# A cached-attention and gated-FFN decode step: kept V tiles, matmuls on constants, and a new last stage

## The chip, the core and the metric

The kernel runs on one core of a Trainium2 chip. The core has five engines that run side by side: PE (TensorE, matrix products), DVE (VectorE, elementwise work and small transposes), ACT (ScalarE, exp and tanh), POOL (GpSimd) and SP (SyncE, which issues the DMAs). The metric is device time in microseconds (us). The time before is 311.15 us, the median of 13 runs (308.57 to 312.18).

## The reference

Four sequences of one token each go twice through the same attention layer and the same feed-forward layer, with the same weights and the same key and value caches.

```python
# B=4 sequences, D=512; 32 query heads, 8 K/V heads, cache length 4096, head size 128; F=1792
def A(x, k_cache, v_cache, wq, wo):
    q = (x @ wq) as [B, 32, 1, 128]
    p = softmax(q @ k^T * 128**-0.5)          # each K/V head serves 4 query heads
    return (p @ v) as [B, 1, 4096] @ wo
def B(x, w_gate, w_up, w_down):
    return (gelu(x @ w_gate) * (x @ w_up)) @ w_down
x = x + A(layernorm(x)); x = x + B(layernorm(x))
x = x + A(layernorm(x)); x = x + B(layernorm(x))
```

Everything is bf16 in memory. One K or V cache is 4 x 8 x 4096 x 128 numbers, 33.6 MB; the weights are 13.9 MB.

## The kernel before

The program is ordered by hand: each engine runs its instructions in the order in which the code names them, and SP issues all DMAs from one queue (`dq`), where an issue that waits for a buffer holds up all later ones.

*Tiles.* The cache of one element (sequence) and one K/V head is cut into two tiles of 128 x 16 x 128, 512 KB each; so K and V have 16 tiles each per element. `KT` has 16 buffers, one for each K tile of an element. V rotates through seven buffers (`KV_BUFS`, `free`), and `held` says which tile lies where.

*Passes.* Each element needs two attention passes, with a feed-forward stage (`dense`) after each. Element b's K tiles are loaded once: they are turned by DVE (L375, `turn`), used for the scores of the first pass, and stay until the scores of the second pass have read them (`scores`, L386). Only then are the buffers loaded with the K tiles of element b+1 (`keys.load`, L368). V is read twice, once in each pass. V tiles are used in the order `order`: all 16 of the first pass of element 0; then for each b the first four of b's second pass, the 16 of the first pass of b+1 and the other twelve of b's second pass; at the end the second pass of element 3. `Values.step` uses one V tile: 16 matmuls of 128 x 32 (L485); then it frees the buffer and calls `load_v` (L464), which asks for the next tiles in that order as long as a buffer is free. `keep` names V tiles that are not freed after the first pass and not loaded again: `KEEP` = 2 tiles, of element 0 only (L450). The first two tiles of a second pass are the last two of the first pass of the same element.

*Stages.* `attend(None, 0)` is the first pass of element 0; all weights are loaded behind its V tiles (`load_rest`: wo in four pieces, wg, wu, and wd in three pieces of 7, 4 and 3 of its 14 columns of blocks). The loop over b then runs `dense(b, 1, ...)`, the feed-forward stage of one element, builds the queries of its second pass, and calls `attend(b, b+1)`: the scores of b's second pass, the loads of K of b+1, and the first pass of b+1. In the dense stages of elements 1 to 3, `fill` steps through the twelve V tiles of the second pass of the element before, between the pieces of the dense stage; in that of element 0 it does nothing. `attend_last` is the second pass of element 3; eight of its V tiles go into K buffers that are free by then. The second feed-forward layer runs once, for all four elements, as `dense(0, B, ...)`, and after it the result is cast, transposed by four matmuls into PSUM (L715), copied (L717) and written out (L718).

*Inside a dense stage:* the end of the output projection (L287), the residual (L294 or L298), the layer norm's sums through one matmul with a constant matrix (L170, L177: the statistics matmul), the reciprocal root by ten small DVE instructions (`ln_rstd`, L186 to L201), the gate and up products (L315 for one element, L308 for four), gelu (L325 to L332, tanh on ACT at L331), `gate_up` (L338, L341), and the down projection (L349, 56 matmuls).

`ROWS` are two PSUM banks for products that come out as rows; `new_scores(0)` and `new_scores(1)` are the two banks of scores.

Of the kernel before, what the change touches and what calls it, by code (L numbers as in the profile page):

```python
# [15 lines left out]
P = 128  # L16
# [3 lines left out]
QD = 4  # L20
# [10 lines left out]
def kernel(  # L31
# [58 lines left out]
    wd_sb = wts.tile([P, KF, D], BF16, name="wd_sb")  # L90
    KT = [[wts.tile([P, CH, Dh], BF16, name=f"kt{i}_{t}") for t in range(NT)] for i in range(Hkv)]
    wq_dram = A_wq.rearrange("(k p) n -> p k n", p=P)
# [6 lines left out]
    q1_bf = state.tile([P, NG, NK, B], BF16, name="q1_bf")  # L99
    xn_bf = state.tile([P, KD, B], BF16, name="xn_bf")  # L100
    qb = state.tile([P, W + NK * 2 * W], BF16, name="qb")

# [12 lines left out]
    def groups(b):  # L115
        return [b % NG, (b + 1) % NG]

    def cache_tile(cache, b, kvh, t):
        return cache[b, kvh].rearrange("(p c) d -> p c d", p=P)[:, t * CH:(t + 1) * CH]

# [4 lines left out]
    def load_rest():  # L125
        n = Hq // 4
        for i in range(4):
            dq.dma_start(out=wo_sb[:, i * n:(i + 1) * n], in_=wo_dram[:, i * n:(i + 1) * n])  # L128
        dq.dma_start(out=wg_sb[:], in_=B_w_gate.rearrange("(k p) n -> p k n", p=P))  # L129
        dq.dma_start(out=wu_sb[:], in_=B_w_up.rearrange("(k p) n -> p k n", p=P))  # L130
        wd_dram = B_w_down.rearrange("(k p) n -> p k n", p=P)
        cuts = [0, KF // 2, KF - 3, KF]
        for lo, hi in zip(cuts, cuts[1:]):
            dq.dma_start(out=wd_sb[:, lo:hi], in_=wd_dram[:, lo:hi])  # L134

    def build_consts():
        nc.vector.memset(mean_f[:], 1.0 / D)
        nc.vector.memset(magic[:], 0x5F3759DF)
        for r in ROWS:
            nc.vector.memset(r[:], 0.0)  # L140
        nc.vector.memset(qb[:], 0.0)
        nc.vector.tensor_reduce(out=amask[:], in_=ident_bf[:].rearrange("p (a i) -> p a i", a=QD),
                                axis=AX.X, op=ALU.max)
        nc.vector.tensor_reduce(out=s32_f[:], in_=ident_bf[:].rearrange("p (a i) -> p i a", a=QD),
                                axis=AX.X, op=ALU.max)
        nc.vector.tensor_copy(out=t32_bf[:],
                              in_=s32_f[:].unsqueeze(1).broadcast_to([P, QD, QS]))
        nc.vector.tensor_reduce(out=hmask[:], in_=s32_f[:].rearrange("p (y h) -> p h y", h=rep),
                                axis=AX.X, op=ALU.max)
        nc.vector.scalar_tensor_tensor(  # L150
            out=dmask[:], in0=amask[:].unsqueeze(2).broadcast_to([P, GH, rep]), scalar=float(D),
            in1=hmask[:].unsqueeze(1).broadcast_to([P, GH, rep]), op0=ALU.mult, op1=ALU.mult)
# [147 lines left out]

    def ffn_in(b0, nb, w_sb, cols):
        bs = slice(b0, b0 + nb)
        rows = new_rows()
        if cols:
            h = rows[:, :KF * nb].rearrange("p (c j) -> p c j", j=nb)
            for c in range(KF):
                for k in range(KD):
                    nc.tensor.matmul(h[:, c], lhsT=w_sb[:, k, c * P:(c + 1) * P],  # L308
                                     rhs=xn_bf[:, k, bs], start=(c == 0 and k == 0),
                                     stop=(k == KD - 1), skip_group_check=True)  # L310
            return h, cols
        for k in range(KD):
            w = w_sb[:, k].rearrange("p (n a i) -> p a n i", a=QD, i=QS)
            for j in range(QD):
                nc.tensor.matmul(rows[j * QS:j * QS + nb, :KF * QS], lhsT=xn_bf[:, k, bs],  # L315
                                 rhs=w[:, j], start=(k == 0), stop=(k == KD - 1))
        return rows, cols

    def ffn_cols(h, nb):
        return h[0] if h[1] else turn_rows(h[0], KF * QS)[:, :, :nb]  # L320

    def gelu(nb, rows, rstd):
        hg = ffn_cols(rows, nb)
        h = small.tile([P, KF, nb], FP32, name="h", tag="h")
        nc.vector.tensor_tensor(out=h[:], in0=hg, in1=spread_rstd(rstd, KF, nb), op=ALU.mult)  # L325
        sq = small.tile([P, KF, nb], FP32, name="sq", tag="sq")
        nc.vector.scalar_tensor_tensor(out=sq[:], in0=h[:], scalar=0.044715, in1=h[:],
                                       op0=ALU.mult, op1=ALU.mult)
        nc.vector.scalar_tensor_tensor(out=sq[:], in0=sq[:], scalar=1.0, in1=h[:],  # L329
                                       op0=ALU.add, op1=ALU.mult)  # L330
        nc.scalar.activation(out=sq[:], in_=sq[:], func=ACT.Tanh, scale=GELU_C)  # L331
        nc.vector.scalar_tensor_tensor(out=h[:], in0=h[:], scalar=0.5,  # L332
                                       in1=spread_rstd(rstd, KF, nb), op0=ALU.mult, op1=ALU.mult)
        return sq, h

    def gate_up(nb, sq, h, rows):
        hu = ffn_cols(rows, nb)
        nc.vector.scalar_tensor_tensor(out=sq[:], in0=sq[:], scalar=1.0, in1=h[:],  # L338
                                       op0=ALU.add, op1=ALU.mult)
        H_bf = small.tile([P, KF, nb], BF16, name="H_bf", tag="H_bf")  # L340
        nc.vector.tensor_tensor(out=H_bf[:], in0=hu, in1=sq[:], op=ALU.mult)  # L341
        return H_bf

    def down(nb, H_bf):
        n = WIDE * rep // nb
        y = ps_sm.tile([P, KD, n, nb], FP32, name="y", tag="sm")
        for c in range(KF):
            for k in range(KD):
                nc.tensor.matmul(y[:, k], lhsT=wd_sb[:, c, k * P:(k + 1) * P],  # L349
# [5 lines left out]
    class Keys:  # L355
# [3 lines left out]
        def tile(self, n):  # L359
            o, u = divmod(n, TG)  # L360
            t, s = divmod(u, GH)
            return groups(self.b)[o] * GH + s, t

        def load(self, count):
            for _ in range(count):
                kvh, t = self.tile(self.nl)
                self.nl += 1
                dq.dma_start(out=KT[kvh][t][:], in_=cache_tile(A_k_cache, self.b, kvh, t))  # L368

# [79 lines left out]
    order += value_order(B - 1, 1)  # L449
    keep = {(0,) + u[2:] for u in value_order(0, 1)[:KEEP]}  # L450
    VB = Hkv * NT
# [5 lines left out]
    def load_v():  # L457
        while free and seen["load"] < seen["upto"]:
# [4 lines left out]
            v = held[b, g, s, t] = free.pop(0)  # L463
            dq.dma_start(out=v[:], in_=cache_tile(A_v_cache, b, g * GH + s, t))  # L464

# [36 lines left out]
    def attend(b2, b1, next_q=None, rest=None):  # L502
# [40 lines left out]
        else:  # L543
            load_wq(0)
            keys.load(TG)
            load_wq(1)
            keys.load(TG)
            load_v()
# [9 lines left out]
            build_q1(0, 0)  # L558
            turn(4)
        sc1 = new_scores(0)  # L560
        scores(sc1, ga, 0)
        turn(4)
        if two:
            vals2.step(max(early[b2] - vals2.n - 1, 0))
        scores(sc1, ga, 1)
        turn()
        p0 = soft(sc1)
# [6 lines left out]
        prob1[ga] = (pe, soft_recip(den))  # L574
        if first:
            q_first(q_rows(0, B, 1), 1, rstd1)
        build_q1(b1, gb)
        turn()
        vals.step(2)
        sc1 = new_scores(0)  # L580
        scores(sc1, gb, 0)
        turn(4)
        vals.step(3)
# [19 lines left out]
        if first:  # L603
# [7 lines left out]
            return (y, OT_bf, heads[3], hp), vals2  # L611
        vals.step(2)
        out_proj(rows, OT_bf, heads[2], hp)
        vals.step()
        out_proj(rows, OT_bf, heads[4], rep, False, True)
        yc = y_rows(rows, 1)
        vals.step()
        y = y_select(yc, 1)
        vals.step()
        return (y, OT_bf, heads[5], rep), vals2  # L620
# [42 lines left out]

    def dense(b0, nb, proj, fill):
        out_proj_end(*proj)
# [5 lines left out]
        fill(1)  # L671
        rg = ffn_in(b0, nb, wg_sb, nb > 1)
        fill(1)
        ru = ffn_in(b0, nb, wu_sb, nb > 1)
        sq, h = gelu(nb, rg, ln_rstd(nb, mv))
        H_bf = gate_up(nb, sq, h, ru)
        fill(2)
        add_y(b0, nb, down(nb, H_bf))

# [3 lines left out]
    for b in range(B):  # L683
        fill = (lambda n: None) if prev is None else prev.step
        dense(b, 1, proj, fill)
        ln_square(b, 1)
# [21 lines left out]

    dense(0, B, proj, lambda n: None)

    xoT = state.tile([P, KD, B], BF16, name="xoT")
    nc.vector.tensor_copy(out=xoT[:], in_=XX[:, 0].rearrange("p b k -> p k b"))
    xo_ps = ps_sm.tile([P, D], BF16, name="xo_ps", tag="sm")
    for k in range(KD):
        nc.tensor.transpose(xo_ps[:B, k * P:(k + 1) * P], xoT[:, k, :], ident_bf[:, :])  # L715
    xo = tmpp.tile([P, D], BF16, name="xo", tag="pp")
    nc.vector.tensor_copy(out=xo[:B, :], in_=xo_ps[:B, :])  # L717
    nc.sync.dma_start(out=out.flatten_outer_dims(), in_=xo[:B, :])  # L718

# [29 lines left out]
```

## Time and profile before

| What | Value |
|---|---|
| median of 13 runs | 311.15 us (308.57 to 312.18) |
| the profiled execution's own time | 311.93 us |
| its span, first to last instruction | 310.2 us |
| mean granted clock of PE | 0.73 of full |
| busy: PE, DVE, ACT | 198.2 us, 170.8 us, 29.1 us |
| DMA | 114.09 MB, mean 368 GB/s |
| issues of K tiles, of V tiles | 64, 118 + 8 of 512 KB |

The profile tells of one execution. A row of the groups gives line, engine, operation, what it writes and reads, how often, busy time, the mean of one in ns, and the engine's idle time ahead of it with what ended it:

```profile
L485 PE MATMUL ot<-pe,v 128*128 128x32 bf16 x1920 | 65.1, 183 | 23.4 <-DMA v<-in_A_v_cache_dram 21.4
L375 DVE STREAM_TRANSPOSE kt<-kt 128x1024 f32<-128x1024 f32 x64 | 75.2, 1217 | 7.1 <-DMA kt<-in_A_k_cache_dram 6.9
...
L386 PE MATMUL sc<-kt,qb 128*32 128x512 bf16 x512 | 55.3, 481 | 17.4 <-DVE kt L375 13.6
```

Busy time says how long an engine had something in work, not how long the program waited for it; PE's matmuls overlap, so the mean of one is longer than the distance from one to the next. The span is told in slices (a digit is a share in tenths), in stretches of time with busy time, granted clock, DMA share and GB/s, and as a chain that is followed back from the last instruction to what released each step.

### The profile page before, as it was taken

To read this page: it belongs to the slowest core of one execution; us is meant where nothing else is said; L and a number is where in the kernel's file an instruction comes from. 1 tells how busy PE (TensorE), PEld (TensorE's weight loads), DVE (VectorE), ACT (ScalarE), POOL (GpSimd) and SP (SyncE) were. 2 spreads that over 40 slices of the span, in tenths; PEclk is the share of its full clock that TensorE was granted. 3 is DMA by queue.
4 is the path that set the end of the run, shared out by engine and by line. 5 is a ranking of instruction groups with operands and counts; after the bars stand their busy time and mean duration, and the time that the engine had idled before them with its cause. 6 is when DMAs were issued, how large, how long until landed. Compare 5 with 4: busy or idle time off the path is not lost.

```text
span 310.2 us, 8714 instructions
## 1 busy us (share of the span) xinstructions
PE 198.2 (64%) x3844; PEld 117.7 (38%) x3844; DVE 170.8 (55%) x481; ACT 29.1 (9%) x70; POOL 0.7 (0%) x6
## 2 busy tenths in 40 slices
PE   1360475343577458788864469799553776997975
PEld 0110244211323125556431346465311454645654
DVE  5585751014247987455588934455598642555143
ACT  0003001000002020300100112000102040003000
POOL 0000000000000000000000000000000000000000
PEclk9999997555558958859955585579755795679685
DMA  7999999999949999999999999999999999999910
GB/s 247 398 412 394 404 411 406 357 367 398 378 165 341 397 413 407 409 405 408 407 408 408 409 407 393 384 389 388 356 413 409 411 408 405 380 362 371 411 76 3
DMA packets 35526, 114.09 MB, mean 368 GB/s; under 512 B 3224, under 2 KB 9120, under 8 KB 35488
## 3 DMA queue, kind: packets, MB, share of 16 engines
q1 hardware_dynamic: 35488, 113.53, 95.0%
q8 instruction: 30, 0.49, 0.6%
q14 instruction: 8, 0.07, 0.1%
HBM read 113.51 MB, written 0.00 MB: 366 GB/s over the span
## 4 chain that ended last, share of the span: by engine, by line
DMA 55%; PE 18%; DVE 14%; SPq 8%; issue 3%; ACT 0%; DVEq 0%; ACTq 0%
DMA v<-in_A_v_cache_dram 29%; DMA kt<-in_A_k_cache_dram 20%; DVE kt L375 5%; PE ot L485 4%; PE sc L386 3%; DMA wd_sb<-in_B_w_down_dram 3%; SPq L128 3%; PE rows L315 3%; SPq L134 3%; PE y L349 3%; DMA kt<-in_A_v_cache_dram 2%; DVE rows L216 1%; PE rows L226 1%; SPq L129 1%; PE st L170 1%
## 5 line engine op out<-in xcount | busy, mean ns | idle before, releaser
L485 PE MATMUL ot<-pe,v 128*128 128x32 bf16 x1920 | 65.1, 183 | 23.4 <-DMA v<-in_A_v_cache_dram 21.4
L375 DVE STREAM_TRANSPOSE kt<-kt 128x1024 f32<-128x1024 f32 x64 | 75.2, 1217 | 7.1 <-DMA kt<-in_A_k_cache_dram 6.9
L485 PEld LDWEIGHTS <-v 128*128 128x128 bf16 x1920 | 58.2, 101 | 53.7 <-DMA v<-in_A_v_cache_dram 32.1
L386 PE MATMUL sc<-kt,qb 128*32 128x512 bf16 x512 | 55.3, 481 | 17.4 <-DVE kt L375 13.6
L216 DVE STREAM_TRANSPOSE rows<-rows 128x512 f32<-128x512 f32 (+1 forms) x23 | 16.3, 707 | 33.5 <-PE rows L226 15.2
L386 PEld LDWEIGHTS <-qb 128*32 128x32 bf16 x512 | 15.9, 105 | 43.4 <-issue 26.6
L493 DVE TENSOR_TENSOR OT_bf<-ot,rden 128x8 bf16<-128x8 f32 (+1 forms) x40 | 6.5, 164 | 39.9 <-PE ot L485 39.7
L405 ACT ACTIVATE pp<-sc,nm 128x512 bf16<-128x512 f32 x16 | 11.0, 687 | 148.1 <-DVE junk L401 117.1
L432 PE MATMUL x<-pp,ident_bf 128*32 128x128 bf16 x256 | 8.0, 256 | 23.6 <-DVE pp L413 23.6
L281 PE MATMUL rows<-wo_sb,OT_bf 128*1 128x512 bf16 (+1 forms) x136 | 14.1, 505 | 7.3 <-DMA wo_sb<-in_A_wo_dram 6.3
L226 PE MATMUL rows<-wq_sb,xn_bf 128*1 128x512 bf16 (+1 forms) x160 | 15.7, 527 | 4.7 <-DMA wq_sb<-in_A_wq_dram 4.4
L432 PEld LDWEIGHTS <-ident_bf 128*32 128x32 bf16 x256 | 5.8, 108 | 28.9 <-issue 26.7
L392 DVE TENSOR_REDUCE m<-sc 128x1 f32<-128x512 f32 x16 | 10.8, 675 | 8.8 <-PE sc L386 8.8
L413 DVE STREAM_TRANSPOSE pp<-pp 128x512 bf16<-128x512 bf16 x16 | 11.2, 700 | 4.7 <-ACT pp L405 4.7
L247 PE MATMUL qe<-qm,t_bf 128*128 128x64 bf16 x16 | 3.4, 213 | 12.9 <-DVE qm L237 7.5
L435 ACT CAST pe<-x 128x512 bf16<-128x512 f32 x16 | 9.4, 586 | 20.8 <-PE x L432 20.8
L349 PE MATMUL y<-H_bf,wd_sb 128*128 128x32 bf16 x280 | 9.6, 192 | 2.6 <-DVE H_bf L341 1.5
L349 PEld LDWEIGHTS <-wd_sb 128*128 128x128 bf16 x280 | 9.0, 101 | 4.0 <-DMA wd_sb<-in_B_w_down_dram 2.9
L250 DVE TENSOR_TENSOR qb<-qe,amask 128x256 bf16<-128x256 f32 x16 | 6.8, 424 | 5.2 <-PE qe L247 5.2
L294 DVE SCALAR_TENSOR_TENSOR XX<-XX,y 128x4 f32<-128x4 f32 x8 | 1.3, 158 | 12.9 <-PE y L349 8.9
L331 ACT ACTIVATE sq<-sq 128x14 f32<-128x14 f32 (+1 forms) x5 | 1.1, 222 | 77.1 <-DVE sq L329 77.1
L315 PE MATMUL rows<-wg_sb,xn_bf 128*1 128x448 bf16 x64 | 6.7, 566 | 2.4 <-DMA wg_sb<-in_B_w_gate_dram 2.4
(78 smaller groups left out, 128.6 us busy)
## 6 DMA issues: line engine op xcount, KB each, us to landing
v<-in_A_v_cache_dram SPq DMA_DIRECT2D x118, 512.0 KB, 8.3
kt<-in_A_k_cache_dram SPq DMA_DIRECT2D x64, 512.0 KB, 10.3
wq_sb<-in_A_wq_dram SPq DMA_DIRECT2D x2, 2048.0 KB, 7.7
wo_sb<-in_A_wo_dram SPq DMA_DIRECT2D x4, 1024.0 KB, 12.0
kt<-in_A_v_cache_dram SPq DMA_DIRECT2D x8, 512.0 KB, 10.4
wg_sb<-in_B_w_gate_dram SPq DMA_DIRECT2D x1, 1792.0 KB, 13.6
wu_sb<-in_B_w_up_dram SPq DMA_DIRECT2D x1, 1792.0 KB
wd_sb<-in_B_w_down_dram SPq DMA_DIRECT2D x1, 896.0 KB, 15.9
```

Of the source, the lines that this page charges most:

```text
L216: nc.vector.transpose(out=rows[:, :n], in_=rows[:, :n])
L226: nc.tensor.matmul(rows[j * QS:j * QS + nb, :], lhsT=xn_bf[:, k, bs], rhs=w, start=(k == 0), stop=(k == KD - 1))
L281: nc.tensor.matmul(rows[r0:r0 + lhsT.shape[-1], :], lhsT=lhsT, rhs=wo_sb[:, i, :], start=(start and n < QD), stop=(stop and n >= hp - QD))
L315: nc.tensor.matmul(rows[j * QS:j * QS + nb, :KF * QS], lhsT=xn_bf[:, k, bs], rhs=w[:, j], start=(k == 0), stop=(k == KD - 1))
L349: nc.tensor.matmul(y[:, k], lhsT=wd_sb[:, c, k * P:(k + 1) * P], rhs=H_bf[:, c, :].unsqueeze(1).broadcast_to([P, n, nb]), start=(c == 0 an ...
L375: nc.vector.transpose(out=words, in_=words)
L386: nc.tensor.matmul(sc[s * QS:(s + 1) * QS], lhsT=qb[:, w0:w0 + 2 * W], rhs=kt[:, :, be // 2, :, be % 2], start=(t == 0 and be == 0), stop= ...
L392: nc.vector.tensor_reduce(out=m[:], in_=sc.rearrange("p c j -> p (c j)"), axis=AX.X, op=ALU.max)
L405: nc.scalar.activation(out=pp[:], in_=sc[:], func=ACT.Exp, bias=nm[:, 0:1], scale=scale, accum_out=ls[:])
L413: nc.vector.transpose(out=flat, in_=flat)
L432: nc.tensor.matmul(x[a * QS:(a + 1) * QS, s], lhsT=ident_bf[:, s * QS:(s + 1) * QS], rhs=pT[:, a], start=True, stop=True, skip_group_check ...
L485: nc.tensor.matmul(self.ot[:, s % 2], lhsT=v[:, i, :], rhs=rhs, start=(c == 0), stop=(c == C - 1), skip_group_check=True)
```

## The change

1. *V tiles.* `keep` holds the first two tiles of the second pass of every element. `loads` gets shorter by six. The last load of V is split in two halves of eight rows each.
2. *Matmuls on constants.* `keep_clock(n)` issues n matmuls of 128 x 512 on the identity and a part of wq into a bank of scores; nobody reads the result. In the dense stage of element 0 `fill` issues 1, 5, 6, 2, 1, 0, 3, 1 of them at its eight places, and two more stand inside the down projection, ahead of its columns 7 and 10. In `attend` of the later elements four stand around the last V tiles of the first pass.
3. *Loads at the start.* The two K tiles of a head share one buffer `KH`, and for element 0 one DMA of 1 MB loads both; they are turned head by head, and the turns stand at other places in `attend`. wd comes in pieces of 7, 3, 3 and 1 columns.
4. *The last stage.* It has code of its own: gate and up products in two halves of seven columns, each half in a bank of its own; gelu and `gate_up` run half by half. The sum with the residual is written as bf16, turned by four DVE transposes of 32 x 32, and written out as 16 rows of 256 bytes. The path for four elements in `ffn_in` goes away.

```diff
-    KT = [[wts.tile([P, CH, Dh], BF16, name=f"kt{i}_{t}") for t in range(NT)] for i in range(Hkv)]
+    KH = [wts.tile([P, C, Dh], BF16, name=f"kt{i}") for i in range(Hkv)]
+    KT = [[KH[i][:, t * CH:(t + 1) * CH] for t in range(NT)] for i in range(Hkv)]
...
-        cuts = [0, KF // 2, KF - 3, KF]
+        cuts = [0, KF // 2, KF - 4, KF - 1, KF]
...
+    def keep_clock(n):
+        if n:
+            idle = new_scores(1).rearrange("p c j -> p (c j)")
+        for _ in range(n):
+            nc.tensor.matmul(idle, lhsT=ident_bf[:, :], rhs=wq_sb[0][:, 0, :512],
+                             start=True, stop=True, skip_group_check=True)
...
-    def down(nb, H_bf):
+    def down(nb, H_bf, between=()):
...
         for c in range(KF):
+            if c in between:
+                keep_clock(between[c])
...
-            t, s = divmod(u, GH)
+            s, t = divmod(u, NT) if self.b == 0 else divmod(u, GH)[::-1]
...
+        def load_whole(self, count):
+            for _ in range(count):
+                kvh = self.tile(self.nl)[0]
+                self.nl += NT
+                dq.dma_start(out=KH[kvh][:], in_=cache_rows(A_k_cache, self.b, kvh, 0, C))
...
-    keep = {(0,) + u[2:] for u in value_order(0, 1)[:KEEP]}
+    keep = {u[:1] + u[2:] for b in range(B) for u in value_order(b, 1)[:KEEP]}
...
-            dq.dma_start(out=v[:], in_=cache_tile(A_v_cache, b, g * GH + s, t))
+            n = CH // 2 if seen["load"] == len(loads) else CH
+            for c in range(0, CH, n):
+                dq.dma_start(out=v[:, c:c + n],
+                             in_=cache_rows(A_v_cache, b, g * GH + s, t * CH + c, n))
...
-        vals.step(2)
+        vals.step()
+        keep_clock(1)
+        vals.step()
         out_proj(rows, OT_bf, heads[2], hp)
         vals.step()
         out_proj(rows, OT_bf, heads[4], rep, False, True)
         yc = y_rows(rows, 1)
         vals.step()
+        keep_clock(1)
         y = y_select(yc, 1)
+        keep_clock(2)
         vals.step()
...
-        fill = (lambda n: None) if prev is None else prev.step
-        dense(b, 1, proj, fill)
+        if prev is None:
+            waits = iter((1, 5, 6, 2, 1, 0, 3, 1))
+            fill = lambda n: keep_clock(next(waits, 0))
+        else:
+            fill = prev.step
+        dense(b, 1, proj, fill, {KF // 2: 1, KF - 4: 1} if prev is None else ())
...
-    dense(0, B, proj, lambda n: None)
...
-    for k in range(KD):
-        nc.tensor.transpose(xo_ps[:B, k * P:(k + 1) * P], xoT[:, k, :], ident_bf[:, :])
...
+    parts = [(0, KF // 2), (KF // 2, KF)]
+    rstd = ln_rstd(B, mv)
+    for i, (c0, c1) in enumerate(parts):
+        ffn_part(wg_sb, hg[i], c0, c1)
+    sq, h, H_bf = ffn_tiles(B)
+    for i, (c0, c1) in enumerate(parts):
+        gelu(B, hg[i][:, c0:c1], rstd, sq[:, c0:c1], h[:, c0:c1])
+    for i, (c0, c1) in enumerate(parts):
+        ffn_part(wu_sb, hu[i], c0, c1)
+        gate_up(hu[i][:, c0:c1], sq[:, c0:c1], h[:, c0:c1], H_bf[:, c0:c1])
+    y = down(B, H_bf)
+    nc.vector.tensor_tensor(out=xo[:, :B * KD].rearrange("p (b k) -> p b k", k=KD),
+                            in0=XX[:, 0], in1=y.rearrange("p k b -> p b k"), op=ALU.add)
+    for a in range(QD):
+        nc.vector.transpose(out=xr[:, a * QS:(a + 1) * QS], in_=xo[a * QS:(a + 1) * QS, :])
```

`ffn_part` holds the loop of matmuls that stood in `ffn_in` for four elements, for a range of columns.

## The prediction

> **What bounds the kernel now.** I read the rows of slices first, then the chain of waits, then SP's timeline and windows of each dense stage.
>
> ```profile
> PEclk9999997555558958859955585579755795679685
> DMA  7999999999949999999999999999999999999910
> GB/s 247 398 412 394 404 411 406 357 367 398 378 165 341 397 413 407 409 405 408 407 408 408 409 407 393 384 389 388 356 413 409 411 408 405 380 362 371 411 76 3
> ...
> DMA 55%; PE 18%; DVE 14%; SPq 8%; issue 3%; ACT 0%; DVEq 0%; ACTq 0%
> ```
>
> The DMA row is full from the second slice to the 38th, with one hole, the slice of about 85 to 93 us, where only 165 GB/s move. The chain is DMA for 55%. So there are three places to look: bytes, the hole, and the tail (the last two slices). One tile of K or V is 512 KB; at the 408 GB/s of the full slices that is **1.285 us**.
>
> The hole, in SP's timeline and in windows of PE (busy, granted clock, DMA share, GB/s):
>
> ```profile
> 75.62 4.32 SPq L464 DMA_DIRECT2D v<-in_A_v_cache_dram  x5
> 91.00 14.82 SPq L368 DMA_DIRECT2D kt<-in_A_k_cache_dram  x16
> ```
>
> ```profile
> 85.20:87.10 1.90, 1.86 (x16) 0.50 0.99 395
> 87.10:88.90 1.80, 0.23 (x1) 0.50 0.43 173
> 88.90:91.00 2.10, 1.92 (x20) 0.50 0.03 8
> 91.00:94.40 3.40, 3.40 (x33) 0.50 0.63 186
> ```
>
> Five V tiles are asked for at 75.62; then no buffer is free until the second-pass scores of element 0 have read the K tiles, at 91.00. The last piece of wd lands at 83.15, so those 7.85 us are the dense stage's own chain, at half clock.
>
> The later dense stages have no such hole. In the chain of waits the first of them (it starts when the last V tile of a first pass is used) ends so:
>
> ```profile
> 133.43 0.55 PE ot L485 x16
> ...
> 147.77 1.13 PE sc L386 x14
> 148.90 7.21 DMA kt<-in_A_k_cache_dram
> ```
>
> The K load is issued at 148.90 but lands 7.21 us later: some five tiles are queued ahead of it.
>
> **Part 1: two V tiles kept for every element (L450).** Element 0's pair is kept already (118 + 8 loads of V = 128 - 2), so elements 1, 2, 3 each lose two loads: 6 x 1.285 = **7.7 us** of DMA, if the DMA stays full. That is the question, since the pair takes two of seven buffers through a dense stage. The stage from the landing of a first pass's last V tile: before, 12 tiles of the older element, four of this element's second pass, one more, then the first K: 18 x 1.285 = 23.1 us; 132.97 + 23.1 = 156.1, and it landed at 156.11. Afterwards 16 x 1.285 = 20.6 us. The K issue, set by compute, doesn't move, and the load needs its bare time, which the trace shows once with an empty queue: issued at 91.00, landed 3.94 us later.
>
> ```profile
> DMA to landing us min/median/max: 3.9/10.3/15.9
> ...
> DMA to landing us min/median/max: 5.5/8.3/12.1
> ```
>
> (K tiles, then V tiles.) Stage 1: due at 153.6, able to land at 148.90 + 3.94 = 152.8. Stage 2: last V 196.44, due 217.0, able at 212.77 + 3.94 = 216.7. Stage 3 (V tiles into freed K tiles): 261.19, due 281.8, able 281.3. All just in time, 0.3 to 0.8 us to spare.
>
> Five rotating buffers: tile n of the stage may be asked for when tile n-5 has been used. Taking the uses of the trace, the first that comes late is the 13th: in stage 2 its buffer is free at 210.3, so it lands at 214.2 and was due at 213.1 (1.1 late); stage 3, 278.7 for 277.9 (0.8); stage 1 in time. The ends are 0 and 1.9 us; I take 1.0, and part 1 is worth **-6.7**.
>
> **Part 2: matmuls on constants.** 21 in the first dense stage, four in each of three attends, of 128 x 512: nearest row L386, x16 in 1.71 to 1.90 us at clock 0.50, but those run on four column groups at once, so one by itself takes about 0.43 us cold, 0.22 warm (worked from 4 x 0.107 and half of it). In the first dense stage 13 of them stand ahead of matmuls that wait for weights (before, 2.4 us for wg, 2.9 for wu, 1.9 for wd): 5 x 0.43 = 2.1, 6 x 0.43 = 2.6, 2 x 0.43 = 0.9, hidden. One ahead of the first statistics matmul has a wait of 0.55, the two inside the down projection have 0.3 to 0.5; of the last five, one stands in the 0.55 ahead of the second statistics matmul, three in the 1.27 ahead of L247, one in the 0.52 ahead of the scores. So even cold they cost about nothing. If nothing hid them, 21 x 0.43 = 9.0.
>
> What they may give: the clock. [...] Against it: the narrow matmuls of the down projection lose the clock again:
>
> ```profile
> 200.00:204.00 4.00, 4.00 (x65) 1.61 (x58) 2.78 (x13) 0.21 (x1) 0.00 (x0) 0.50 1.03 413
> 204.00:208.00 4.00, 3.73 (x116) 3.48 (x116) 1.44 (x11) 0.00 (x0) 0.00 (x0) 0.93 1.01 382
> 208.00:212.00 4.00, 3.62 (x73) 1.91 (x69) 3.17 (x16) 0.00 (x0) 0.00 (x0) 0.64 1.02 379
> ```
>
> Warm at 204, back to 0.64 after 56 such matmuls, though PE reads as busy. I take it that the fillers bridge it. With a warm clock, on the chain 83.15 to 94.4: statistics matmul 0.56 to 0.37 (the row at 143.21), scores 1.90 to 0.95, q rows 1.71 to 0.95, second scores 1.71 to 0.90: together 2.7. The q rows at 85.2 give nothing: DVE's rstd chain ends at 87.39, after them. And wd is cut so that the last piece holds 1 column of 14, not 3: 4 matmuls behind it, not 12: 0.57 to 0.2, **-0.35**. DVE works from 97 to 121 almost without a wait and starts from those scores, so the whole first attend moves by what they move. Ends -0.35 (cold) and -3.1; I take **-2.6**.
>
> In the later attends one filler stands ahead of the 13th V tile (PE waited there 0.15 and 0.43), one under DVE's turn (hidden), two ahead of the 16th, 0.86 cold, 0.3 of it a wait in stage 2. So +0.6 to +1.2 on the chain when cold, against the gate and up rows (1.66 to 0.85 each) and q rows when it warms the stage. The chain has 0.3 to 0.8 to spare: **0**, ends -1 and +1.5 over all three.
>
> **Part 3: the head.** K of element 0 comes in 1 MB loads, transposed head by head. Bytes and order of groups are the same, V is used on landing (37.79, landed 37.74), everything until 83 waits for DMA: 0, ends -0.5 and +0.5.
>
> **Part 4: the tail**, 298.6 to 310.2, all on the path:
>
> ```profile
> 302.98 0.22 DVE L325 TENSOR_TENSOR h<-rows,rstd 128x56 f32<-128x56 f32 x1
> ...
> 304.37 0.22 DVE L341 TENSOR_TENSOR H_bf<-rows,sq 128x56 bf16<-128x56 f32 x1
> 304.64 1.65 PE L349 MATMUL y<-H_bf,wd_sb 128*128 128x32 bf16 x56 [0.41 <-DVE H_bf L341]
> 306.33 0.17 DVE L298 TENSOR_TENSOR XX<-XX,y 128x16 f32<-128x16 f32 x1 [1.74 <-PE y L349]
> ...
> 306.76 0.59 PE L715 MATMUL xo_ps<-ident_bf,xoT 128*4 128x128 bf16 x4 [0.47 <-DVE xoT L712]
> 307.39 0.41 DVE L717 COPY xo<-xo_ps 4x512 bf16<-4x512 bf16 x1 [0.68 <-PE xo_ps L715]
> ```
>
> DVE starts at 302.98 because rstd ends then, not because it waits for the gate rows. Halving the tiles therefore doubles its instructions: 10 steps of about 0.22 (between 0.20 at 14 elements and 0.25 at 56) until the first half of H_bf, 305.2 for 304.6: **+0.55**. The output loses cast, four transposes on PE and copy (1.5 us from 306.33 to the issue at 307.83) for one add and four turns of 32 x 32 (nearest row: the turn of 128 x 32, 0.21): 0.2 + 4 x 0.22 = 1.1: **-0.4**. The last V tile in halves: the 16th use waits for y's matmuls until 298.05, and the tile landed at 298.00: 0. Sum +0.2, ends -0.3 and +0.6.
>
> **Sum.** -6.7 - 2.6 + 0.2 = -9.1. The profiled execution took 311.93 (span 310.2): 302.8. It lies 0.8 above the median of 13 runs, 311.15, by slow DMA stretches that come and go; I give half of that: **302.5**.
>
> **Rivals.**
> A. The forecast, own range 300 to 305: 0.55.
> B. The clock stays or falls to half before the scores at 89 us: only -0.35 there, 311.9 - 6.7 - 0.35 + 0.2 = 305.1. For it: the row at 208. Against it: the wide fillers. 0.24.
> C. The bytes go, but DMA idles instead in the dense stages, as K issue is compute's: with 1.5 us more chain in each stage 4.5 of the 7.7 are lost and B's clock with it: 309. For it: 0.3 to 0.8 us of slack. Against: warm stages are shorter. 0.11.
> D. Slower: five buffers starve the DMA. If the 7 to 8 us from issue to landing were the DMA's own and not queueing, with four in flight (the fifth being read) a tile would take 7.5 / 4 = 1.9 us, 0.6 over 1.285, for 14 tiles in three stages: +25 - 10 = 327. It decides once the bare time of a load exceeds 4 x 1.285 = 5.1 us; the trace shows 3.94 once. 0.07.
> Within 0.3% (what a measurement tells from no change): between C and D, 0.03.
>
> Range 299.5 to 308.5: A, B and most of C. Faster 0.90, same 0.03, slower 0.07.
>
> **What would show it.** Right: 120 loads of V; DMA at 400 or more in the three dense stages, first K landing 20 to 21 us after the last V of a first pass; first K issue near 89.5 and clock 1.00 there; down matmuls of the last stage starting at +0.5 relative to rstd. Wrong: V loads issued on use with SP waiting for PE while DMA falls under 9 tenths (C, D), clock 0.5 at the first second-pass scores (B), or the filler's matmuls directly ahead of matmuls whose data had landed.

## The result, and the profile after

| | before | after |
|---|---|---|
| median | 311.19 us (48 runs, 308.57 to 316.01) | 308.21 us (11 runs, 304.39 to 310.31) |
| ratio, 95% interval | | 0.9877 [0.9851, 0.9903] |
| profiled execution, its span | 311.93, 310.2 us | 309.84, 308.1 us |
| bytes moved | 114.09 MB | 110.94 MB |
| V loads | 118 + 8 | 112 (the last in halves) + 8 |

The changed kernel is faster by 3.0 us between the medians, and by 3.8 by the ratio. The medians are of all runs, and the ratios, here and below, leave out the runs that lie more than 1.5% above the fastest of their kernel. The forecast was 302.5, a gain of 8.65 from the 311.15 known then. The profiled execution of the changed kernel lay 1.6 us above its median, so the two spans differ by 2.1 only.

The bytes went as forecast: 3.15 MB less, six tiles. The time for them did not. These are the rows of slices of the changed kernel:

```profile
PEclk9998576557897559997955597589755795679685
DMA  6999999999949999999999999899999999889910
GB/s 249 427 412 424 411 420 411 357 378 386 398 150 362 408 415 417 416 395 313 361 411 410 417 419 416 312 312 355 407 407 413 410 368 375 287 298 411 411 54 3
```

The DMA row shows nearly the same nines as before. The row below it has three new troughs: 395, 313, 361 in slices 18 to 20, then 312, 312, 355, then 287, 298. Before, these places stood at 405 to 408, at 384 to 389, and at 380 and 362. They are the dense stages of elements 1, 2 and 3. In windows over the three stages (start and end, length, PE busy, granted clock, DMA share, GB/s), before:

```profile
139.00:148.00 9.00, 7.45 (x203) 0.99 1.03 407
200.00:208.00 8.00, 7.73 (x174) 0.71 1.02 397
264.00:272.00 8.00, 7.75 (x176) 0.69 1.00 379
```

and after:

```profile
139.00:148.00 9.00, 8.24 (x173) 0.81 0.92 301
200.00:208.00 8.00, 7.08 (x184) 0.87 0.94 311
264.00:272.00 8.00, 7.70 (x191) 0.81 0.89 305
```

A fifth to a quarter of the rate is gone, at a share of 0.9. An engine that is busy with a slow packet counts as busy: in the first of these windows a packet of 4 KB took 198 ns on average, 163 before; nearly one in ten took over 300 ns, and these made up 23% of the packets' time. Only the bytes tell. The DMA view of the first stage (132 to 154 us after, 136 to 157 before) gives issues, KB each and the median time from issue to landing. Before, then after:

```profile
v<-in_A_v_cache_dram SPq DMA_DIRECT2D x9, 512.0 KB, 7.4
```

```profile
v<-in_A_v_cache_dram SPq DMA_DIRECT2D x10, 512.0 KB, 6.0
```

The V loads land sooner after their issue, yet fewer are under way. Counted from the two traces, 5.5 loads on average were issued and not landed from 139 to 149 us before, and 4.0 from 135 to 146 us after (a quarter of the loads have no landing in the trace, so this is an estimate). With some 7.1 and 6.2 us from issue to landing, 5.5 x 0.524 MB / 7.1 us is 406 GB/s, and 4.0 x 0.524 / 6.2 is 341. This only says that the three numbers fit together; that the buffers set the depth, and the depth the rate, is for an experiment (`e3`). The first K load of the stage, issued at 145.94, took 7.59 us to land; in stages 2 and 3 it took 7.89 and 7.51. Before they took 7.21, 8.23 and 7.74.

Where the 2.1 us of the span come from, by the traces: the last piece of wd lands at 81.31 us for 83.15 before, **-1.84**; from there to the first K issue of element 1 6.60 us for 7.85, **-1.25**; from that issue to the last V use of element 1's first pass 43.07 for 42.37, **+0.70**; from there to the last V use of all 165.10 for 164.69, **+0.41**; the tail 11.98 for 12.10, **-0.12**. In this pair of executions all of the gain is there at 131 us, and the three stages from which six loads were taken brought nothing.

That last stretch differs much between executions, so one pair can't settle it. In a second trace of the changed kernel (`e16`, 303.39 us, the shortest of its seven runs) it took 157.9 us, with the troughs at 343 to 378 GB/s. `e12` and `e14`, one and the same kernel, took 157.8 and 162.9. Over all traces it took 159.7 to 165.6 us (mean 163.3) in the seven that keep nothing of the elements 1 to 3 (`e3` aside, with 169.3), and 157.9 to 165.1 (mean 162.4) in the six that keep two tiles of each. What keeping is worth is therefore read from the times of many runs.

### The profile page after: what moved, and what is told of

Same layout as the page of the kernel before. It is cut to its first block, busy times and chain, and to the rows that moved or that the text cites. A ratio compares the mean times of both kernels' runs of the same rounds, so it can differ in the third digit from the quotient of the medians.

```text
span 308.1 us, 8759 instructions
## 1 busy us (share of the span) xinstructions
PE 200.4 (65%) x3865; PEld 118.5 (38%) x3873; DVE 172.5 (56%) x490; ACT 29.4 (10%) x71; POOL 0.7 (0%) x6
## 2 busy tenths in 40 slices
DMA packets 33694, 110.94 MB, mean 360 GB/s; under 512 B 3060, under 2 KB 8952, under 8 KB 32632
## 4 chain that ended last, share of the span: by engine, by line
DMA 47%; PE 25%; DVE 15%; SPq 9%; issue 3%; ACT 0%; DVEq 0%
DMA v<-in_A_v_cache_dram 25%; DMA kt<-in_A_k_cache_dram 19%; PE ot L501 6%; PE sc L399 5%; SPq L134 3%; DMA wd_sb<-in_B_w_down_dram 3%; DVE kt L388 3%; SPq L140 3%; PE y L356 3%; DVE rows L223 3%; PE rows L314 2%; PE rows L233 2%; PE rows L288 2%; DVE qb L257 1%; PE st L177 1%
## 5 line engine op out<-in xcount | busy, mean ns | idle before, releaser
L288 PE MATMUL rows<-wo_sb,OT_bf 128*1 128x512 bf16 (+1 forms) x136 | 13.1, 473 | 7.4 <-DMA wo_sb<-in_A_wo_dram 6.4
L233 PE MATMUL rows<-wq_sb,xn_bf 128*1 128x512 bf16 (+1 forms) x160 | 14.9, 504 | 4.5 <-DMA wq_sb<-in_A_wq_dram 4.1
L346 PE MATMUL sc<-wq_sb,ident_bf 128*128 128x512 bf16 x25 | 10.3, 483 | 0.2 <-issue 0.2
## 6 DMA issues: line engine op xcount, KB each, us to landing
kt<-in_A_k_cache_dram SPq DMA_DIRECT2D x8, 1024.0 KB, 15.5
```

The source lines that it names most:

```text
L233: nc.tensor.matmul(rows[j * QS:j * QS + nb, :], lhsT=xn_bf[:, k, bs], rhs=w, start=(k == 0), stop=(k == KD - 1))
L288: nc.tensor.matmul(rows[r0:r0 + lhsT.shape[-1], :], lhsT=lhsT, rhs=wo_sb[:, i, :], start=(start and n < QD), stop=(stop and n >= hp - QD))
L346: nc.tensor.matmul(idle, lhsT=ident_bf[:, :], rhs=wq_sb[0][:, 0, :512], start=True, stop=True, skip_group_check=True)
```

## The experiments

Sixteen kernels. The ratios are against the kernel before on the same chip, with 95% intervals.

### Keeping, and buffers, each alone

`e1` is the changed kernel with only element 0's pair kept, 118 + 8 V loads again; all else stays:

```diff
-    keep = {u[:1] + u[2:] for b in range(B) for u in value_order(b, 1)[:KEEP]}
+    keep = {(0,) + u[2:] for u in value_order(0, 1)[:KEEP]}
```

`e2` is the kernel before with the opposite edit alone. `e3` is the kernel before with all its loads, but in the dense stages of elements 1 to 3 two V buffers are set aside until the second pass begins: used as the kept pair would be, with no load saved. `e4` is the changed kernel without the twelve fillers in the attends.

```diff
+                if last and parked:
+                    if self.n == 1:
+                        free.extend(parked)
+                        parked.clear()
+                if not last and (b, g, s, t) in park:
+                    parked.append(held.pop((b, g, s, t)))
```

(the core of `e3`, with the rest of its edit left out; `park` is the pair of each of the elements 1 to 3.)

> The changed kernel with only element 0's pair of V tiles kept: 126 tiles of V are loaded again, 12 not 14 times with five rotating buffers. Starvation theory (a DMA stream needs some six tiles in flight for its full rate, and the pair leaves five buffers): the three dense stages go back to about 400 GB/s and the time is 307.5 to 309.5, next to the changed kernel's 308.2. Rival, that the six loads do save their 7.7 us and something else gives them back: 314 to 316.

> The kernel before with one edit, two V tiles of every element kept. Starvation theory: DMA falls to 250 to 330 GB/s in the dense stages of elements 1 to 3, and the gain is 0 to 2 us (309 to 311). The prediction's working: minus 6.7 us (304.5).

> The kernel before with its 126 loads of V, but the two buffers of the last two V tiles of a first pass (elements 1 to 3) lie idle until the second pass begins: five rotating buffers in the dense stages and nothing saved. Starvation theory: 4 to 8 us slower than before (315 to 319), at 250 to 350 GB/s in those stages. Rival, that five buffers are enough, as the prediction worked out from a bare load of 3.94 us: at most 2 us slower (311 to 313).

> The changed kernel without the twelve matmuls on constants in the attends of the later elements. Theory that these stand on the chain and delay the K loads of stages 2 and 3 by 1 to 1.9 us: 304.5 to 306. Starvation theory alone: 307.5 to 309.

| run | median us (before 311.93) | ratio |
|---|---|---|
| e1, keeping undone | 309.81 | 0.9898 [0.9856, 0.9940] |
| e2, keeping alone | 310.97 | 0.9989 [0.9947, 1.0031] |
| e3, two buffers parked, no load saved | 318.30 | 1.0214 [1.0160, 1.0267] |
| e4, no fillers in attends | 308.53 | 0.9839 [0.9758, 0.9921] |

Keeping by itself gives no gain that can be measured, and undoing it costs none. `e3` has the other half of the account, and came as the starvation theory expected: two buffers fewer in the dense stages cost 6.4 us (6.7 by the ratio), where six loads at 1.285 us are worth 7.7. The windows of `e2` over the same stages show that the change's other parts have no share in the troughs:

```profile
139.00:148.00 9.00, 7.61 (x193) 0.96 0.94 314
200.00:208.00 8.00, 7.76 (x179) 0.72 0.93 317
264.00:272.00 8.00, 6.81 (x182) 0.88 0.88 293
```

and `e3`, whose stages lie later, has them without any change of the bytes:

```profile
139.00:149.00 10.00, 8.44 (x214) 0.93 0.91 323
203.00:213.00 10.00, 8.69 (x215) 0.89 0.98 347
266.00:276.00 10.00, 9.69 (x220) 0.79 0.97 362
```

One expectation of `e1` was missed. With all seven buffers rotating again, the rate was to return to about 400 in all three stages. It did in the first only:

```profile
GB/s 256 428 413 421 412 423 410 356 380 384 399 146 380 411 415 414 386 382 412 412 413 411 416 417 377 386 358 350 415 407 413 416 419 417 375 313 417 410 40 3
```

In the second stage it stayed at 350 to 386, in the third at 313 to 375. From 203 to 213 us some five loads were under way and only 323 GB/s moved, again with one packet in sixteen over 300 ns. So fewer buffers make such troughs, as `e3` shows, but they are not the only thing that does; what else does is open.

`e4` lies where the changed kernel lies: no effect of the fillers in the attends is seen, and its interval of some 2.5 us on either side leaves room for a small one.

### The other parts alone

`e5` is the kernel before with the 1 MB loads of element 0's K and the turns head by head; `e6` is it with the 21 fillers of the first dense stage and wd in four pieces; `e7` is the changed kernel with `KEEP = 1`; `e8` is the kernel before with the K loads, the first stage's fillers and the new output (gelu in one piece), one kept tile for the elements 1 to 3, and no filler in the attends.

```diff
-            keys.load(TG)
+            keys.load_whole(GH)
...
-        cuts = [0, KF // 2, KF - 3, KF]
+        cuts = [0, KF // 2, KF - 4, KF - 1, KF]
...
-KEEP = 2
+KEEP = 1
```

(a line of `e5`, of `e6`, and all of `e7`.)

> The kernel before with one edit: element 0's K in eight loads of 1 MB, turned head by head. Theory that the longer rows of these loads run faster: the last piece of wd lands near 81.3 us, not 83.1, and the time falls by 1.5 to 2 us (about 310). Rival, that the 81.3 of the changed kernel came from elsewhere (its V loads, or the chip): wd near 83 and no change.

> The kernel before with the 21 matmuls on constants in the dense stage of element 0, and wd in four pieces. Theory that a shorter chain there moves all that follows: first K issue 6.6 us after the last piece of wd (7.85 before), and 1 to 1.5 us off the time (310.5). Rival, that the shift is lost again in the stage behind it: the issue moves and the time doesn't (311 to 312).

> The changed kernel with one tile kept for every element, not two: 124 loads of V, six rotating buffers. Starvation theory: what a stage saves (1.3 us) and what the sixth buffer costs are again nearly equal, with a rate of 350 to 390 GB/s in the dense stages: 307.5 to 309.5, no different from keeping two (308.2). Rival, that the full rate returns with six buffers: 305 to 306.5.

> The kernel before with element 0's K in 1 MB loads, the filled dense stage of element 0, the new output (bf16 sum, four DVE turns, 16 rows) but gelu in one piece, two tiles kept of element 0 and one of each other element; no matmuls on constants in the attends. If the parts add up: 311.9 - 1.7 - 1.2 - 0.4 - 1 = 307.6, and if one kept tile pays in full 305. The changed kernel's 308.2 is to be beaten by the 0.55 us of the halved gelu at least.

| run | median us (before 312.48) | ratio |
|---|---|---|
| e5, 1 MB K loads | 311.92 | 0.9956 [0.9917, 0.9994] |
| e6, fillers in the first dense stage, wd cut | 311.20 | 0.9975 [0.9940, 1.0010] |
| e7, changed kernel, one kept tile an element | 306.41 | 0.9806 [0.9761, 0.9850] |
| e8, the parts together, one kept tile | 308.07 | 0.9823 [0.9769, 0.9877] |

In `e5` the last piece of wd lands at 82.14, 1.0 us earlier than before (81.3 was expected, and about 310 us of time): its second slice moves 426 GB/s, where the kernel before has 398. `e7` came out at its rival's time, 305 to 306.5, but not for its rival's reason: the full rate did not return, its first stage is at 365, 287 and 377. On one chip (below) one kept tile brings nothing. In `e6` the stage behind that landing takes 6.59 us for 7.85, as in the changed kernel. The timeline of `e6` (start, length) shows why:

```profile
84.93 1.82 PE L226 MATMUL rows<-wq_sb,xn_bf 128*1 128x512 bf16 x16 [0.33 <-DVE mv L174]
...
86.69 1.46 PE L348 MATMUL sc<-wq_sb,ident_bf 128*128 128x512 bf16 x3
...
88.83 1.07 PE L395 MATMUL sc<-kt,qb 128*32 128x512 bf16 x16
89.52 0.76 PEld L226 LDWEIGHTS <-xn_bf 128*1 128x1 bf16 x16
89.73 1.08 PE L226 MATMUL rows<-wq_sb,xn_bf 128*1 128x512 bf16 x16
```

The first q rows still run cold, 1.82 us for sixteen; the scores behind the fillers run warm, 1.07 for 1.90, and the next q rows 1.08. The shift shows in every trace, though not in one size. From the landing of wd to the first K issue of element 1 the six traces without these fillers took 7.86 or 7.87 us, the twelve with them 6.58 to 7.44. The four longest (`e4`, `e11`, `e13` and `e16`) found the clock at half again just ahead of the scores (0.50 or 0.51 from 86 to 88 us in `e4` and `e16`, 0.98 in the first trace of the changed kernel), and those sixteen took 1.38 to 1.69 us. What the shift is worth in the time, 0.8 us, lies within the interval of `e6`, and its 311.20 is in the range of its rival, under which the issue moves and the time doesn't.

### A part that the diff doesn't name

The changed kernel, `e1`, `e4`, `e7` and `e8` had V packets of 159 ns (median of the 4 KB packets; before and after, from 176 to 188 us, where V alone loads), the kernel before, `e2`, `e3`, `e5` and `e6` 162. What differs is the place of the V buffers in SBUF: byte 193,760 of a partition before, 194,048 after, since the two small tiles of the new output come ahead of them. The second is a multiple of 256, the first isn't a multiple of 64. `e9` is the kernel before with an unused tile of 32 bytes, which puts V on 193,792; `e10` has tiles of 96 and 192 bytes, which put the weights, K (126,368 before) and V on multiples of 256; `e11` is the changed kernel with 32 bytes that take V off again; `e12` is `e8` with everything on multiples of 256.

```diff
+    pad = state.tile([P, 16], BF16, name="pad")
```

(the whole edit of `e9`, and of `e11`.)

> The kernel before with one unused tile of 32 bytes ahead of the V buffers, whose start moves from 193760 to 193792, a multiple of 256 bytes. Theory that the changed kernel's V loads run faster (packets of 159 ns, not 162) only because its two new small tiles moved the V buffers to a multiple of 256: 159 ns here too, 417 not 408 GB/s over V, and 126 tiles x 0.028 us = up to 3.5 us less (308.5). Rival, that whole K loads or the chip's memory did it: 162 ns and 312.

> The kernel before with unused tiles of 96 and 192 bytes, so that weights, K and V all start at multiples of 256 bytes. Alignment theory: K packets go to 159 ns too, and 1 to 1.8 us come off beyond e9 (307). Rival: K stays at 162 to 164 ns, same as e9.

> The changed kernel with an unused tile of 32 bytes ahead of the V buffers, so that they start 32 bytes past a multiple of 256. Alignment theory: V packets 162 ns, the last piece of wd 0.5 to 1 us later (82 to 82.3), time 2 to 3 us up (310 to 311), so that hardly more than 1 us of the change is left. Rival: as the changed kernel, 308.2.

> The kernel of e8 with weights and K moved to multiples of 256 bytes as well (V stays on one). Alignment theory: 1 to 2 us less than e8 (306 to 307), and below the changed kernel by 1.5 to 2.

| run | median us (before 311.32) | ratio |
|---|---|---|
| e9, V on 256 | 309.60 | 0.9938 [0.9899, 0.9976] |
| e10, weights, K and V on 256 | 306.80 | 0.9875 [0.9829, 0.9921] |
| e11, changed kernel, V off 256 | 309.70 | 0.9883 [0.9844, 0.9922] |
| e12, e8 with all on 256 | 302.85 | 0.9726 [0.9680, 0.9772] |

The same window, which loads V alone, before, in `e9` and in `e10`:

```profile
176.00:188.00 12.00, 8.56 (x178) 0.78 1.03 408
```

```profile
176.00:188.00 12.00, 9.38 (x183) 0.68 1.03 418
```

```profile
176.00:188.00 12.00, 9.74 (x184) 0.64 1.02 417
```

Thirty-two unused bytes are worth 2% of the rate, 408 to 418, though with 1.9 us by the ratio only about half of the time that was expected of `e9`, and in `e10` the K packets too fall from 161 to 164 ns to 159. `e11` had its packets at 162 ns and wd's landing at 82.34 (81.31 with V in place), as expected, and its time was to be 310 to 311. Its twelve runs spread from 305.29 to 312.27; the median, 309.70, is 1.6 us under the kernel before, but the ratio is that of the changed kernel. So the rate is shown, and undoing the place of V did not show a loss of time inside the changed kernel. `e12` is shorter than the 306 to 307 expected of it; the last piece of wd lands at 79.1 to 79.3 in it and in the three runs of its base below, two us earlier than in the changed kernel.

### Kept tiles once more, on one chip

`e12` is under both kernels, so the question of keeping was put again on that base, where nothing but the number of kept tiles of the elements 1 to 3 differs; beside them the changed kernel.

```diff
-    keep = {(b,) + u[2:] for b in range(B) for u in value_order(b, 1)[:(KEEP if b == 0 else 1)]}
+    keep = {(0,) + u[2:] for u in value_order(0, 1)[:KEEP]}
```

(`e13` from `e14`, which is `e12` again; `e15` keeps `[:KEEP]` of every element.)

> The kernel of e12 (all buffers on multiples of 256 bytes, 1 MB loads of the first K, filled dense stage of element 0, new output) with no tile kept of elements 1 to 3. If one kept tile pays in full, three loads of 1.26 us more than e14: 306.5 when e14 is at 302.8.

> The kernel of e12 again, one tile kept of each of the elements 1 to 3, as the middle of three: 302 to 303.5.

> The kernel of e12 with two tiles kept of every element. Starvation theory: the second tile pays nothing, or costs: e14 plus 0 to 2 us, with 3 to 4 tiles in flight in the dense stages. The prediction's working: e14 minus 3 us (five buffers are enough).

> The changed kernel itself beside these three: 1.0 to 1.5% under the kernel before, as on its first chip, and over e15 by 3 us or so (K and weights not aligned, gelu in halves).

| run | median us (before 311.68) | ratio |
|---|---|---|
| e13, none kept | 302.83 | 0.9721 [0.9683, 0.9758] |
| e14, one | 304.10 | 0.9749 [0.9711, 0.9788] |
| e15, two | 302.47 | 0.9696 [0.9648, 0.9744] |
| e16, the changed kernel | 307.72 | 0.9863 [0.9819, 0.9908] |

The intervals of none, one and two overlap: no effect of keeping that can be measured. Between none and two the medians differ by 0.4 us, where the prediction's working gives 6.7. The three comparisons (`e2` with before, `e1` with the changed kernel, `e13` with `e15`) put two kept tiles 0.3 to 0.8 us ahead by their ratios, none of it clear of the intervals. The rows of slices and of packets show how the same time comes about, `e13` and then `e15`:

```profile
GB/s 239 431 421 431 413 421 415 383 405 404 411 147 354 403 419 417 417 415 389 404 407 415 417 418 416 416 415 415 401 412 418 417 418 416 417 398 398 398 17 3
DMA packets 34414, 114.09 MB, mean 379 GB/s; under 512 B 3140, under 2 KB 9032, under 8 KB 33352
```

```profile
GB/s 247 433 419 434 410 419 414 384 408 401 413 142 396 418 420 417 418 384 296 379 401 415 421 416 368 368 263 389 373 409 418 420 416 418 338 283 418 416 63 3
DMA packets 33550, 110.94 MB, mean 367 GB/s; under 512 B 3044, under 2 KB 8936, under 8 KB 32488
```

Behind slice 13 the row without kept tiles falls under 397 in one slice, to 389; with two tiles kept it has three troughs, down to 296, 263 and 283. 3.15 MB less, moved 3% slower. `e12` to `e15` beat both kernels: some 302.5 to 304 us, 2.5 to 3% under the kernel before, and `e13` does it with the old rule for keeping. The changed kernel lies 5.3 us above `e15`, where 3 was expected; two of these are the earlier landing of wd, the rest was not taken apart.

## Why the prediction was right and wrong

**Part 1, keeping (-6.7): the step that failed.** That six tiles go, 3.15 MB, was right, and so is 1.285 us for each at the full rate. The failed step is "the load needs its bare time, ... landed 3.94 us later", with what was built on it: stage 1 "able to land at 148.90 + 3.94", the first late tile "the 13th", the price "0 and 1.9 us; I take 1.0". The 3.94 was read from a load into an empty queue. In the stage the first K loads needed 7.5 to 7.9, V loads 6.0, and the price of two buffers, which `e3` measured with all loads left in, is 6.4 us where 1.0 was taken. Part 1 comes to 0.3 us by `e2` (interval -1.6 to +1.0 as a change of the time), not 6.7. The count of buffers asked whether a tile is requested soon enough after its buffer is free; it did not ask what rate four tiles under way carry. Why single packets get slow then, and why they did in two stages of `e1` with all buffers rotating, stays open.

**Rival D** had this mechanism, five buffers that starve the DMA, and its point: "once the bare time of a load exceeds 4 x 1.285 = 5.1 us". With four under way a load took 6.0, though a bare one took 3.94 before, and the K load issued at 87.91 in the changed kernel 4.53: the condition held for loads that share the queue, not for a lone one. D's price of 25 us was too high: it let 14 tiles in each stage cost 0.6 more, while the troughs are 9 to 13 us of a stage of some 22. Over 11 us, 341 for 406 GB/s is 1.8 us a stage, 5.3 in three. **Rival C**, with 309, came nearest in value, by luck. Its reason, a K issue that comes late because compute sets it, isn't what happened: the K issue stood 15.0, 15.9 and 16.7 us behind the last V use of the stage, before 15.5, 16.3 and 15.9, and the V tiles ahead of it were slow already.

**Part 2, fillers (-2.6): the mechanism held in part, the size didn't.** Ahead of the K issue the working has 0.35 + 0.19 + 0.95 = 1.5 (wd's last piece, a statistics matmul, the scores); measured 1.25, with the scores warm at 1.11 us and the q rows at 82.92 cold at 1.88. That the fillers raise the clock and hold it through the narrow down matmuls was the author's estimate; no trace of the kernel before shows it, and no run shows the 2.6. In the first trace of the changed kernel the granted clock was 0.98 from 72 to 82 us, where the kernel before had 0.50, then 0.50 from 84 to 86 and 0.98 from 86 to 88: it did not hold behind the down matmuls. Nor do these lose it each time: in the dense stage of element 1 in the kernel before it was 1.00 from 140 to 148 us, with the 56 down matmuls at 140.75 and q rows at 143.91 of 1.10 us. In four of the twelve traces with these fillers the clock came up only in the scores, as rival B had it in part, and 0.4 to 0.75 was left. What failed is the rest, 1.1 us for the second q rows and scores, under "the whole first attend moves by what they move". Both ran warm, 1.09 and 1.11, and the attend didn't get shorter. From the K issue on, it waits for bytes. Windows behind that issue, before:

```profile
91.00:97.00 6.00, 5.48 (x65) 0.68 0.72 216
97.00:109.00 12.00, 6.50 (x118) 0.98 1.02 404
109.00:121.00 12.00, 7.33 (x127) 0.60 1.03 412
```

and after:

```profile
87.91:94.00 6.09, 4.52 (x82) 1.00 0.62 170
94.00:106.00 12.00, 7.72 (x98) 0.60 1.02 402
106.00:118.00 12.00, 7.50 (x127) 0.55 1.03 415
```

After six microseconds the DMA is full in both. So the moment of the issue counts, and the bytes behind it. From the issue to the last V use of this attend it took 41.3 to 44.5 us in the eighteen traces, so the 0.70 more of this pair is within what executions differ by. In the time `e6` has -0.8. The fillers of the later attends: 0 forecast, none seen in `e4`.

**Part 3, the head (0, ends -0.5 and +0.5): wrong.** "Bytes and order of groups are the same" is true and doesn't settle it. wd landed 1.84 us earlier. 1 MB loads are 1.0 of it (`e5`); the place of the V buffers, which no line of the diff names, fits the rest (`e9` -0.6, `e11` 1.0 by its undoing), and its higher rate goes on through the V loads behind (418 GB/s from 176 to 188 us in `e9`, 408 before).

**Part 4, the tail (+0.2): right.** The lines after:

```profile
301.01 0.19 DVE L323 TENSOR_TENSOR h<-rows,rstd 128x28 f32<-128x28 f32 x1
...
303.07 1.65 PE L356 MATMUL y<-H_bf,wd_sb 128*128 128x32 bf16 x56 [0.81 <-DVE H_bf L340]
303.07 1.54 PEld L356 LDWEIGHTS <-wd_sb 128*128 128x128 bf16 x55 [0.87 <-issue]
303.21 0.19 DVE L340 TENSOR_TENSOR H_bf<-sc,sq 128x28 bf16<-128x28 f32 x1
304.76 0.17 DVE L764 TENSOR_TENSOR xo<-XX,y 128x16 bf16<-128x16 f32 x1 [1.36 <-PE y L356]
304.96 0.84 DVE L767 STREAM_TRANSPOSE xr<-xo 32x32 bf16<-32x32 bf16 x4
305.83 0.35 SPq L768 DMA_DIRECT2D out_dram<-xr  x1
```

From h to the down products 2.06 us, 1.66 before: +0.40 for the forecast +0.55. From those to the output's issue 2.76, 3.19 before: -0.43 for -0.4.

**The sum.** As ratios of 311.19, the parts alone are: keeping -0.3, 1 MB K loads -1.4, fillers of the first stage -0.8, V on 256 bytes -1.9; together -4.4, for -3.8 measured by the ratio (interval -4.6 to -3.0). Each of the four has some 1.2 us of interval on either side, so this agrees but proves no finer division, and `e11` did not repeat the 1.9 inside the changed kernel. The direction was right, for half wrong reasons, and that 308.2 lies inside the range of 299.5 to 308.5 is luck: of the sum, 3.3 of 4.4 come from two edits that were costed at nothing, and the one that was to bring most brought none that can be measured.

## What to carry to other kernels

A kept tile is a buffer taken from the loads, so price both: the bytes saved, and the rate at the depth that is left, which is the bytes under way over the landing time in that stage, not a lone load's landing time: here 4.0 x 0.524 MB over 6.2 us, where a lone load had 3.94 us. Read the bytes per slice and not only the busy share, since slow packets count as busy (here a share of 0.92 at 301 GB/s). Don't divide a gain by one pair of traces: here one kernel took 157.8 and 162.9 us for the same stretch. When a diff adds a tile, see where it moves the buffers behind it: here 32 unused bytes made 418 GB/s of 408.

## What the hardware showed that was not expected

- **Depth.** Loads of 512 KB, 95 to 292 us, mean rate by the number under way, counted from the traces (rounded, since a quarter of the landings is missing): before, some 390 GB/s at 5 and 400 from 6 to 8; after, some 300 at 3 (20 us), 350 at 4 (20 us) and 410 from 6 on; in `e3` some 340, 350, 370 to 390 and 400 from 3 to 6. It is no strict law: `e6`, `e9` and `e13` had 6 to 12 us at four under way with 390 to 410, and `e1` had 323 with five. In the shallow stretches the median packet of 4 KB stays at 159 ns, and single packets of over 300 ns, up to 2.2 us, make up a sixth to a quarter of the packets' time. Why is open. A buffer more for V, the direct test from the other side, was not run.
- **Place of a buffer.** A V packet of 4 KB took 162 ns in the kernel before, where the V buffers start at byte 193,760, and 159 ns in the changed kernel, where they start at 194,048, a multiple of 256. With 193,792 in `e9`, also a multiple, 418 GB/s moved in a window of V alone, 408 before; V, K and weights on multiples of 256 took 1.25% off the time [0.8, 1.7] in `e10`. What makes the difference no run shows, and 64 or 128 bytes were not told apart.
- **Size of a load.** From 4 to 12 us 1 MB loads of K moved 425 GB/s in `e5`, where little else differs but the order of the tiles, and 428 in the changed kernel; 512 KB loads moved 398.
